# Attention scores on the two row halves of TensorE, memory products on whole tiles, and the order of a step around them

## The chip, the cores and the metric

One core of one Trainium2 chip. The metric is the device time of one launch in microseconds (us); the median of three runs of the kernel before is 1613.03 us. The engines are called by their names in the profile: PE is TensorE's matmuls and PEld its weight loads, DVE is VectorE, ACT is ScalarE, POOL is GpSimd, SP is the engine that issues the DMAs.

## The reference

Two branches read the same 2048 x 576 input `x`; a gate per row mixes them.

```python
g = sigmoid((x * gate_w).sum(-1, keepdims=True))
out = g * A(x) + (1 - g) * B(x)
B = (gelu(x @ w_gate) * (x @ w_up)) @ w_down          # 576 -> 4608 -> 576
# A: 32 heads of 18, four segments of 512 rows, in order
for s in range(4):
    p = softmax(q_s @ k_s.T * 18**-0.5 + mask)        # mask: keys ahead of the query
    a_dot = p @ v_s
    a_mem = (phi(q_s) @ M) / (phi(q_s) @ z + 1e-6)    # phi(t) = t + 1 or exp(t)
    o_s = sigmoid(beta) * a_mem + (1 - sigmoid(beta)) * a_dot
    M += phi(k_s).T @ v_s ; z += phi(k_s).sum(rows)
A = concat(o) @ wo
```

The mask leaves, for each of a segment's four query tiles of 128 rows (qi = 0 to 3), (qi + 1) x 128 keys.

## The kernel before, in words

Numbers are kept in pairs of 16-bit words (a high part and what is left), so most products come as several matmuls. Four stretches follow one another.

**Start and projections** (L594 to L823). The first segment's rows of `v` are made in full precision by `first_words`; the weights' scales come from sums of squares (`stat_v`, `stat_qk`, `scale_sum`, which sums over partitions by a small matmul at L90 into the bank that `spare` gives out). For each segment s, `vrows` makes the value rows, `project` makes nine tiles of columns (q in tiles 0 to 4, k in 4 to 8: tile 4 is shared, 64 rows each), and `put_columns` keeps phi of them. Every segment but the first also works on the memory of the one before, tile of 128 rows by tile (q): `key_rows` (L553) turns phi(k) to rows with transposes on TensorE, from tile 4's upper 64 rows on; `memorize` (L564) multiplies them with the values into two banks, where the fifth span of columns has 64 columns only; `keep_memory` (L574) masks that to head blocks in `bd`; `recall` (L517) multiplies phi(q) with `bd` into two banks of 16 heads each, so that the span that holds head 14 to 21 is cut in two and the fifth span has 64 rows only; `put_recall` (L534) divides and stores. Closures in the list `later` hold the second halves of these steps, and `finish_later` runs them; so the place of that call sets the order on VectorE.

**The main loop** (L1104, `step(v)`, 72 steps). A step is one tile of 128 hidden columns f for one half of the rows: V, X and Y are three banks (tags V, G, U), filled by seven half-products (`product`, `rest`, `low_rests`). Each step also does eight chains of the down projection of the block before (`down`, L977: six matmuls at L985, then one VectorE instruction at L991 or L993 that adds the bank to `acc`), in order: five `early` chains, one each after products X, S2 and A12 and two behind the even scores, then three `late` chains behind the fourth product (S4). A chain's bank comes from `spare()`, which in the loop means the two banks of tag `dn`. And each step carries one head of attention, with a lag of two steps:

- `scores(2k)` behind the first pair of low rests and `scores(2k+1)` at the end of the step. Its four query tiles are matmuls of 54 rows (three words of 18): qi = 3 on rows 0 to 53 in one `st` bank, qi = 2 and qi = 0 on rows 64 to 117 in the other, qi = 1 on rows 0 to 53 in a `dn` bank. `put(a, i)` (L896) reads piece i on VectorE: it adds the mask, keeps a copy in SBUF and the row maximum.
- `powers`, `pair_rows`, `turn_rows`: exponentials on ScalarE, the high and low words, and two transposing DMAs on SP's queue from `ph` to `pt` (two buffers each).
- `values(a)`: twenty matmuls of 37 columns at L940 into the bank `pv`; `normalize(k)`: five VectorE instructions (L950 to L957) that read `pv`. There is one `pv` bank, so the next head's `values` wait for it.

`end_pair` at the start of a step multiplies the two hidden tiles of the step before (L1007 on VectorE, from banks G and U) and splits them (L1011, L1012). The order on TensorE, ScalarE, VectorE and GpSimd is that of the code (`manual_schedule`); SP's queue is ordered by the compiler. PSUM is eight banks: G, U, V, pv, two `st`, two `dn`. A tag with two buffers gives a new tile the buffer that comes free first.

**The tail** finishes the last block's chains and the product with `wo`.

In the tile names of the profile `gl` is a gelu tile, `hh` its pair, `pairg` and `paird` are pairs of weights, `pf` the scores in SBUF, `mx` their maxima, `ob` the rows of a group of heads.

Of the kernel before, what the change touches and what calls it, by code (L numbers as in the profile page):

```python
# [8 lines left out]
F32 = mybir.dt.float32  # L9
# [9 lines left out]
P = 128  # L19
# [18 lines left out]
SPANS = [(128 * j, min(128, D - 128 * j)) for j in range(KT)]  # L38
HEADS = [(a // DH, (a + w - 1) // DH + 1) for a, w in SPANS]


@with_exitstack
def kernel(ctx: ExitStack, tc: tile.TileContext, xs, wqk, wv, wo, wgu, wd, beta, out):
# [346 lines left out]
    with tc.tile_pool(name="prj", bufs=2, side="right", reuse_waits="tile") as pp:  # L390
# [25 lines left out]
        def square_sum(o, r, on_act):  # L416
            if on_act:
                junk = pa.tile([P, D], F32, name="krow", bufs=2).bitcast(BF16)
                act.activation(junk[:, : r.shape[1]], r, AF.Square, accum_out=o)
            else:  # L420
                sum_squares(o, r)
# [4 lines left out]
        def stat_qk(j):  # L426
            square_sum(wst[:, 10 + j : 11 + j], raw_qk[:, j], j % 2)
# [89 lines left out]
        def recall(s, q, banks=(("st", 2), ("st", 2))):  # L517

            na, nb = (bank(*i) for i in banks)
            for j, (a, w) in enumerate(SPANS):  # L520
                h0, h1 = HEADS[j]
                for o, lo in ((na, 0), (nb, 16)):
                    g0, g1 = max(h0, lo), min(h1, lo + 16)
                    if g0 >= g1:
                        continue
                    last = (j == 2 and lo == 0) or j == KT - 1
                    first = j == 0 or (j == 2 and lo == 16)
                    pe.matmul(o[:, (g0 - lo) * MC : (g1 - lo) * MC],
                              phi[s, j][:w, q * P : (q + 1) * P],
                              bd[:w, j, (g0 - h0) * MC : (g1 - h0) * MC],  # L530
                              start=first, stop=last, skip_group_check=True)
            later.append(lambda: put_recall(s, q, na, nb))

        def put_recall(s, q, na, nb):  # L534
# [3 lines left out]
            for b, o in enumerate((na, nb)):  # L538
                o3 = o[:, : 16 * MC].rearrange("p (h d) -> p h d", d=MC)
                dve.tensor_scalar(dn[:, 16 * b : 16 * b + 16].unsqueeze(2), o3[:, :, DH:], 1e-6, None, OP.add)  # L540
            rd = pp.tile([P, H], F32, name="rden", bufs=2)
            mo = pp.tile([P, D], F32, name="mo", bufs=2)
            dve.reciprocal(rd, dn)
            dve.tensor_tensor(rd, rd, gh[:, 0], OP.mult)
            for b, o in enumerate((na, nb)):
                o3 = o[:, : 16 * MC].rearrange("p (h d) -> p h d", d=MC)
                dve.tensor_tensor(
                    mo[:, b * NH : (b + 1) * NH].rearrange("p (h d) -> p h d", d=DH),
                    o3[:, :, :DH],
                    rd[:, 16 * b : 16 * b + 16].unsqueeze(2).to_broadcast([P, 16, DH]), OP.mult)  # L550
            sp.dma_start(oms[hf][t * P : (t + 1) * P, :], mo)

        def key_rows(s, q):  # L553
            ka, kb = bank("st", 2), bank("V")
            tok = slice(q * P, (q + 1) * P)
            pe.transpose(ka[:, 0:64], phi[s, 4][64:, tok], ident[64:, 64:])
            for i in range(3):
                pe.transpose(ka[:, 64 + i * P : 64 + (i + 1) * P], phi[s, 5 + i][:, tok], ident)
            pe.transpose(kb[:, :P], phi[s, 8][:, tok], ident)
            k = kr[s, q] = pa.tile([P, D], F32, name="krow", bufs=2)  # L560
            act.activation(k[:, :448], ka[:, :448], AF.Copy)
            act.activation(k[:, 448:], kb[:, :P], AF.Copy)

        def memorize(s, q):  # L564
# [3 lines left out]
            for j, (a, w) in enumerate(SPANS):  # L568
                h0, h1 = HEADS[j]
                o = mem[s][j // 3][:w, (j % 3) * 8 * MC : (j % 3) * 8 * MC + (h1 - h0) * MC]  # L570
                pe.matmul(o, k[:, a : a + w], v[:, h0:h1].rearrange("p h d -> p (h d)"),
                          start=q == 0 and j % 3 == 0, stop=q == 3 and j in (2, 4), skip_group_check=True)

        def keep_memory(s):  # L574
            ka, kb = mem.pop(s)
            n = 8 * MC
            for o, d, k in ((ka[:, : 3 * n], flat(bd[:, 0:3]), flat(bdm[:, 0:3])),
# [4 lines left out]
                else:  # L582
                    m = pa.tile([P, D], F32, name="krow", bufs=2)[: o.shape[0], : o.shape[1]]
# [10 lines left out]
        with tc.manual_schedule(engines=ORDERED):  # L594
# [34 lines left out]
            stat_qk(4)  # L629
            low_x(0, 1)  # L630
            for j in (6, 5, 8, 7):
                stat_qk(j)
            finish_later()
            low_x(0, 2)
# [198 lines left out]
    with tc.tile_pool(name="keep", bufs=2, side="right", reuse_waits="tile") as kp, ExitStack() as tail:  # L833
# [262 lines left out]
        def end_pair():  # L1096

            for g in ends:
                hidden(*g)
# [229 lines left out]
```

## Time and profile before

| | |
|---|---|
| median of 3 runs | 1613.03 us (1612.63 to 1613.62) |
| the profiled execution's own time | 1610.65 us |
| its span | 1608.9 us |
| busy: PE, PEld | 1596.7, 933.5 us |
| busy: DVE, ACT, POOL | 1140.2, 1161.9, 1133.1 us |
| mean granted clock of TensorE | 0.998 |
| score matmuls (L888) | 4 x 128, of 512, 384, 256 and 128 columns |
| DMA queue 1 | 206.92 MB, 71.6% of 16 engines |

Lines of a timeline read: start (us from the span's start), length, engine, line of the code, operation, tile written <- tiles read, shape, count of instructions merged into the row; in brackets the engine's idle time before it and what ended it. Matmuls overlap: a row's start says when one began, the start of the next when it made room; the length includes the way through the array. A busy PE is therefore not yet a PE at its peak, and the spacing of starts is what is added up here. In the table of stretches the columns are the stretch, its length, the busy time (and count) of PE, PEld, DVE, ACT and POOL, the granted clock of TensorE, the busy share of the DMA engines and GB/s.

### The profile page before, as it was taken

How to read it: one execution, taken by the hardware profiler on the slowest of the kernel's cores; microseconds unless marked ns; L12 is line 12 of the kernel's file. 1: busy time of each engine (PE TensorE's matmuls, PEld its weight loads, DVE VectorE, ACT ScalarE, POOL GpSimd, SP SyncE). 2: the span in 40 equal slices, each digit the busy share in tenths (PEclk: the TensorE clock that was granted, in tenths of full speed). 3: DMA queues.
4: the chain of work that ended last, by engine and by line, in shares of the span. 5: the costliest groups of instructions: out<-in, count | busy, mean ns of one | idle time of the engine just before them, and what ended most of it. 6: DMA issues, size and time to landing. Idle time of an engine off the chain costs nothing.

```text
span 1608.9 us, 32610 instructions
## 1 busy us (share of the span) xinstructions
PE 1596.7 (99%) x11924; PEld 933.5 (58%) x11924; DVE 1140.2 (71%) x2940; ACT 1161.9 (72%) x1966; POOL 1133.1 (70%) x1093
## 2 busy tenths in 40 slices
PE   9999999999999999999999999999999999999999
PEld 5656754555555555555555555555555555555577
DVE  6665785677777777777777777777777777765543
ACT  6665445888888888888888888878888888864200
POOL 2233647798987888887979778888879797785200
PEclk9999999999999999999999999999999999999999
DMA  6532443788978797988988887978798887846251
GB/s 240 193 109 77 149 142 82 124 133 131 138 120 141 122 144 120 143 126 140 134 135 133 131 139 123 148 128 141 129 140 137 133 133 129 127 74 155 59 133 60
DMA packets 471872, 209.00 MB, mean 130 GB/s; under 512 B 427552, under 2 KB 436768, under 8 KB 471200
## 3 DMA queue, kind: packets, MB, share of 16 engines
q1 hardware_dynamic: 471712, 206.92, 71.6%
q8 instruction: 94, 1.54, 0.4%
q14 instruction: 66, 0.54, 0.1%
HBM read 90.99 MB, written 27.26 MB: 73 GB/s over the span
## 4 chain that ended last, share of the span: by engine, by line
PE 96%; DVE 1%; DMA 1%; POOL 1%; ACT 1%; issue 0%; SPq 0%; DVEq 0%; POOLq 0%
PE dn L985 26%; PE U L1025 17%; PE V L1025 12%; PE G L1025 11%; PE pv L940 4%; PE st L322 3%; PE st L312 3%; PE dn L322 2%; PE G L312 2%; PE U L1032 2%; PE st L888 2%; PE V L1037 1%; PE G L1037 1%; PE U L312 1%; PE G L1032 1%; PE V L1032 1%
## 5 line engine op out<-in xcount | busy, mean ns | idle before, releaser
L920 POOL TENSOR_TENSOR ph<-pf,ph 128x512 f16<-128x512 f32 (+1 forms) x256 | 354.2, 1405 | 176.9 <-ACT ph L919 175.0
L985 PE MATMUL dn<-paird,hh 128*128 128x288 f16 x3396 | 476.7, 286 | 0.9 <-POOL paird L305 0.9
L1025 PEld LDWEIGHTS <-pairg 128*128 128x128 f16 x3024 | 285.3, 98 | 309.9 <-issue 16.0
L985 PEld LDWEIGHTS <-hh 128*128 128x128 f16 x3456 | 332.3, 98 | 138.1 <-issue 2.6
L993 DVE SCALAR_TENSOR_TENSOR acc<-dn,ev,acc 128x288 f32<-128x288 f32 x534 | 274.0, 516 | 95.7 <-PE dn L985 86.9
L909 ACT ACTIVATE pf<-pf,mb,esc 128x512 f32<-128x512 f32 (+3 forms) x512 | 292.9, 642 | 6.7
L1025 PE MATMUL G<-x,pairg 128*128 128x512 f16 x864 | 209.9, 379 | 0.5 <-DVE gl L1007 0.5
L1025 PE MATMUL U<-xt,pairg 128*128 128x512 f16 x864 | 210.1, 379 | 0.0
L1012 POOL TENSOR_TENSOR hh<-gl,hh 128x512 f16<-128x512 f32 x144 | 164.0, 1160 | 56.0 <-ACT hh L1011 56.0
L896 DVE CUSTOM_DVE_ANT_0 pf<-st,mask 128x512 f32<-128x512 f32 (+2 forms) x384 | 184.0, 504 | 0.0
L293 POOL TENSOR_TENSOR pairg<-raw,pairg 128x640 f16<-128x640 f32 (+2 forms) x144 | 173.9, 1229 | 10.6 <-ACT pairg L289 10.6
L919 ACT ACTIVATE ph<-pf 128x512 f16<-128x512 f32 (+1 forms) x256 | 172.4, 720 | 0.0
L1162 DVE COPY gl<-U 128x512 f32<-128x512 f32 x72 | 49.8, 691 | 137.2 <-PE U L1025 137.2
L289 ACT ACTIVATE pairg<-raw 128x640 f16<-128x640 f32 (+2 forms) x144 | 89.5, 648 | 70.7 <-POOL raw L283 41.2
L258 POOL TENSOR_SCALAR raw<-raw,sc 128x640 f32<-128x640 f32 x72 | 135.0, 1889 | 0.0
L1015 ACT ACTIVATE gl<-gl,sc 128x512 f32<-128x512 f32 x144 | 98.3, 717 | 45.4 <-DVE gl L1181 25.2
L1025 PE MATMUL V<-x,pairg 128*128 128x512 f16 x432 | 106.0, 381 | 0.4 <-ACT hh L1011 0.2
L1181 DVE TENSOR_TENSOR gl<-U,gl 128x512 f32<-128x512 f32 x72 | 49.7, 691 | 79.8 <-PE U L1037 72.5
L1025 PE MATMUL V<-xt,pairg 128*128 128x512 f16 x432 | 105.7, 381 | 0.0
L1025 PE MATMUL U<-x,pairg 128*128 128x512 f16 x432 | 105.0, 379 | 0.4 <-DVE gl L1181 0.4
L1011 ACT ACTIVATE hh<-gl 128x512 f16<-128x512 f32 x144 | 82.9, 616 | 25.2 <-DVE gl L1007 25.1
L906 ACT ACTIVATE mb<-mx,esc 128x4 f32<-128x4 f32 x128 | 37.8, 295 | 85.8 <-DVE mx L896 83.1
(271 smaller groups left out, 2565.1 us busy)
## 6 DMA issues: line engine op xcount, KB each, us to landing
raw<-in_wgu_dram SPq DMA_DIRECT2D x36, 640.0 KB
rawd<-in_wd_dram SPq DMA_DIRECT2D x36, 288.0 KB
qk<-stage SPq DMA_DIRECT2D x36, 256.0 KB
qt<-qk SPq DMA_DIRECT2D x128, 72.0 KB
kt<-qk SPq DMA_DIRECT2D x128, 72.0 KB
vp<-vstage SPq DMA_DIRECT2D x16, 296.0 KB
vt<-vp SPq DMA_DIRECT2D x16, 296.0 KB
qt<-qk SPq DMA_DIRECT2D x128, 36.0 KB
```

What stands on the lines that cost most here:

```text
L258: pool.tensor_scalar(r, r, scl[f // 2][0][:, 0:1], None, OP.mult)
L293: pool.tensor_tensor(spot(f, *p, 1), raw_g[f][:, p[0] : p[1]], spot(f, *p, 0), OP.subtract)
L312: pe.matmul(o, w(k, a), x[:, 4 * b + k], start=n == 0, stop=False)
L896: dve.tensor_tensor_reduce(prob[a][:, COL[qi] : COL[qi + 1]], ov, mask[:, L - (qi + 1) * P :], 1.0, -3e38, OP.add, OP.max, mx[a][:, qi : q ...
L909: act.activation(r, r, AF.Exp, bias=b[:, qi : qi + 1], scale=esc[:, 0, c : c + 1])
L919: act.activation(h[:, 0, cols], p[:, cols], AF.Copy)
L920: pool.tensor_tensor(h[:, 1, cols], p[:, cols], h[:, 0, cols], OP.subtract)
L985: pe.matmul(o[:, :NH], hh[:, a, q * P : (q + 1) * P], w[:, b, n * NH : (n + 1) * NH], start=i == 0, stop=i == 5)
L993: dve.scalar_tensor_tensor(av, o[:, :NH], ev, av, OP.mult, OP.add)
L1012: pool.tensor_tensor(hh[:, 1], t, hh[:, 0], OP.subtract)
L1015: act.activation(t, o, AF.Gelu_apprx_tanh, scale=scl[f // 2][0][:, 2 + c : 3 + c])
L1025: pe.matmul(o, w[:, i, (a + k) * P : (a + k + 1) * P], x[:, b + k], start=start and k == 0 and i == 0 and b == h, stop=k == 1 and i == 1, ...
```

## The change

1. **Scores.** The four query tiles get a bank each: 3 and 2 in `st`, 1 and 0 in `dn`. Tiles 3 and 0 are on the lower rows (640 columns together), tiles 2 and 1 on the upper (640).
2. **Order in a step.** VectorE reads pieces 0 and 1 first, as they hold `dn` banks: those of the even scores right behind them, those of the odd scores in `end_pair`, between the two hidden tiles. `values(2k-3)` moves from the first half of the step to behind the even scores, `normalize(k-2)` from the middle of the step to behind the last piece of the even scores, `values(2k-2)` from behind the even scores to behind the late chains. In step 4 alone (the fifth) the first early chain moves to the second one's place.
3. **Memory.** `recall` uses all 128 rows and whole spans: three spans in one bank, two in the other. Head 21 then lies in both; `put_recall` copies its 19 columns from the second bank and adds them to the first. `key_rows` transposes six whole tiles, `memorize` uses 128 columns for each span. The mask `bdm` is in BF16, the unused rows of `bd` are set to zero, `krow` is 640 columns wide.
4. **Start.** The square sum of tile 6 moves to ScalarE. `finish_later` is cut into single calls. The scale of the q and k weights is made behind the first two value tiles' first halves on ScalarE, its sum goes to a `dn` bank, bank G is freed ahead of the first weight pair, and the third low part of `x` comes later.

```diff
 def stat_qk(j):
-    square_sum(wst[:, 10 + j : 11 + j], raw_qk[:, j], j % 2)
+    square_sum(wst[:, 10 + j : 11 + j], raw_qk[:, j], j in (1, 3, 5, 6, 7))
...
 def recall(s, q, banks=(("st", 2), ("st", 2))):
     na, nb = (bank(*i) for i in banks)
-    for j, (a, w) in enumerate(SPANS):
-        h0, h1 = HEADS[j]
-        for o, lo in ((na, 0), (nb, 16)):
-            g0, g1 = max(h0, lo), min(h1, lo + 16)
...
-            pe.matmul(o[:, (g0 - lo) * MC : (g1 - lo) * MC],
-                      phi[s, j][:w, q * P : (q + 1) * P],
-                      bd[:w, j, (g0 - h0) * MC : (g1 - h0) * MC],
-                      start=first, stop=last, skip_group_check=True)
+    for j, (h0, h1) in enumerate(HEADS):
+        o, lo = (na, 0) if j < 3 else (nb, HS)
+        pe.matmul(o[:, (h0 - lo) * MC : (h1 - lo) * MC], phi[s, j][:, q * P : (q + 1) * P],
+                  bd[:, j, : (h1 - h0) * MC], start=j in (0, 3), stop=j in (2, 4), skip_group_check=True)
...
 def put_recall(s, q, na, nb):
+    both = na[:, HS * MC : (HS + 1) * MC]
+    dve.tensor_copy(mo[:, :MC], nb[:, :MC])
+    dve.tensor_tensor(both, both, mo[:, :MC], OP.add)
...
 def key_rows(s, q):
-    pe.transpose(ka[:, 0:64], phi[s, 4][64:, tok], ident[64:, 64:])
-    for i in range(3):
-        pe.transpose(ka[:, 64 + i * P : 64 + (i + 1) * P], phi[s, 5 + i][:, tok], ident)
-    pe.transpose(kb[:, :P], phi[s, 8][:, tok], ident)
-    k = kr[s, q] = pa.tile([P, D], F32, name="krow", bufs=2)
-    act.activation(k[:, :448], ka[:, :448], AF.Copy)
-    act.activation(k[:, 448:], kb[:, :P], AF.Copy)
+    for i in range(4):
+        pe.transpose(ka[:, i * P : (i + 1) * P], phi[s, 4 + i][:, tok], ident)
+    for i, j in ((0, 8), (1, 4)):
+        pe.transpose(kb[:, i * P : (i + 1) * P], phi[s, j][:, tok], ident)
+    k = kr[s, q] = pa.tile([P, KT * P], F32, name="krow", bufs=2)
+    act.activation(k[:, :448], ka[:, 64:], AF.Copy)
+    act.activation(k[:, 448:], kb[:, :192], AF.Copy)
...
 def memorize(s, q):
-        o = mem[s][j // 3][:w, (j % 3) * 8 * MC : (j % 3) * 8 * MC + (h1 - h0) * MC]
-        pe.matmul(o, k[:, a : a + w], v[:, h0:h1].rearrange("p h d -> p (h d)"),
+        o = mem[s][j // 3][:, (j % 3) * 8 * MC : (j % 3) * 8 * MC + (h1 - h0) * MC]
+        pe.matmul(o, k[:, a : a + P], v[:, h0:h1].rearrange("p h d -> p (h d)"),
...
-            stat_qk(4)
+            for j in (4, 5, 6, 8, 7):
+                stat_qk(j)
+            later.pop(0)()
             low_x(0, 1)
-            for j in (6, 5, 8, 7):
-                stat_qk(j)
-            finish_later()
-            low_x(0, 2)
+            later.pop(0)()
...
                     if qs[0] and k == 1:
-                        scale_sum(0, wst[:, 10:19])
-                        make_qk(0)
                         put_rows(0, 0, 1, vb[0], usc, 1.0)
                         put_rows(0, 1, 1, vb[1], usc, 1.0)
+                        turns.update(of=2)
+                        scale_sum(0, wst[:, 10:19])
+                        turns.update(of=3)
+                        later.pop(2)()
+                        make_qk(0)
+                        low_x(0, 2)
                         finish_later()
...
-        PIECES = (((3,), 0), ((2, 0), 64), ((1,), 0))
+        PIECES = ((3, 0, "st"), (2, 64, "st"), (1, 64, "dn"), (0, 0, "dn"))
...
+            for qi, r, tag in PIECES:
+                n, h = (qi + 1) * P, slice(r, r + 3 * DH)
+                out[qi] = bank(tag, 2)[:, :n]
+                pe.matmul(out[qi], q[h, e * L + qi * P : e * L + n], kt[h, e * L : e * L + n], start=True, stop=True)
...
         def end_pair():
             for g in ends:
                 hidden(*g)
+                if g is ends[0]:
+                    for qi in (0, 1):
+                        if puts:
+                            puts[max(puts)](qi)
...
         def step(v):
...
             product(X, f, A11, x1, 0, 4, True)
-            put(2 * k - 1, 0)
+            put(2 * k - 1, 3)
             dve.tensor_copy(Y, X)
...
-            some(fb - 1, early[:1])
-            put(2 * k - 1, 1)
+            if v != 4:
+                some(fb - 1, early[:1])
             put(2 * k - 1, 2)
             puts.pop(2 * k - 1, None)
-            if on(k - 2):
-                values(2 * k - 3)
...
-            some(fb - 1, early[1:2])
+            some(fb - 1, early[0 if v == 4 else 1 : 2])
...
-            if on(k - 2):
-                normalize(k - 2)
             product(X, f, A12, x1, 2, 6)
...
             if on(k):
                 puts[2 * k] = scores(2 * k)
+            put(2 * k, 0)
+            put(2 * k, 1)
             dve.tensor_tensor(g1, Y, g1, OP.add)
             gelu(f, e, g1, g1)
...
-            put(2 * k, 2)
             if fb:
                 dve.tensor_tensor(g0, V, g0, OP.add)
                 gelu(f, c, g0, g0)
-            if on(k - 1) and fb:
-                values(2 * k - 2)
+            if on(k - 2):
+                values(2 * k - 3)
             some(fb - 1, early[3:4])
-            put(2 * k, 0)
+            put(2 * k, 3)
             some(fb - 1, early[4:])
-            put(2 * k, 1)
+            put(2 * k, 2)
             puts.pop(2 * k, None)
+            if on(k - 2):
+                normalize(k - 2)
...
             product(Y, f, S4, x2_, 2, 6)
             rest(Y, f, UG, x2_, (0,) if fb else (0, 1))
             some(fb - 1, late[:1])
...
             some(fb - 1, late[1:])
-            if on(k - 1) and not fb:
+            if on(k - 1):
                 values(2 * k - 2)
```

49 lines of the change are left out of this document (18 added, 31 removed).

## The prediction

> **What bounds the kernel now.** I read the page's head and its chain that ended last, then the table of busy time by stretch, then the timelines of TensorE and VectorE over one step of the main loop, at last VectorE's waits.
>
> ```profile
> span 1608.9 us, 32610 instructions
> ...
> PE 96%; DVE 1%; DMA 1%; POOL 1%; ACT 1%; issue 0%; SPq 0%; DVEq 0%; POOLq 0%
> ```
>
> TensorE is 96% of the chain. Its own queue is the time; any other engine matters only where TensorE must wait for it. So I look at one step in the middle, and ask how much room each wait leaves. TensorE (S below is the start of the even head's scores, 808.66):
>
> ```profile
> 797.21 1.47 PE L1025 MATMUL V<-xt,pairg 128*128 128x512 f16 x6
> ```
>
> ```profile
> 808.44 0.39 PE L1037 MATMUL U<-x,pairg 64*128 64x512 f16 x1
> 808.66 0.38 PE L888 MATMUL st<-kt,qt 54*128 54x512 f16 x3
> 808.88 0.27 PE L888 MATMUL dn<-kt,qt 54*128 54x256 f16 x1
> 809.08 0.67 PE L940 MATMUL pv<-vt,pt 128*128 128x37 f16 x20
> 809.60 1.63 PE L985 MATMUL dn<-paird,hh 128*128 128x288 f16 x12
> 811.07 1.46 PE L1025 MATMUL U<-x,pairg 128*128 128x512 f16 x6
> ...
> 812.58 2.40 PE L985 MATMUL dn<-paird,hh 128*128 128x288 f16 x18
> ...
> 815.56 1.47 PE L1025 MATMUL V<-xt,pairg 128*128 128x512 f16 x6
> ```
>
> The step lasts 18.35 us (797.21 to 815.56) and no row of it carries idle time. Six matmuls of a chain take 0.735 (twelve from 809.60 to 811.07), so the three late chains begin at 812.58, 813.31 and 814.05. VectorE beside it:
>
> ```profile
> 805.22 0.46 DVE L950 TENSOR_REDUCE pv<-pv 128x144 f32<-128x288 f32 x1
> ...
> 806.63 0.30 DVE L957 TENSOR_TENSOR ob<-ob,pv 128x144 f32<-128x144 f32 x1
> 807.03 0.52 DVE L993 SCALAR_TENSOR_TENSOR acc<-dn,ev,acc 128x288 f32<-128x288 f32 x1
> 808.87 0.69 DVE L1181 TENSOR_TENSOR gl<-U,gl 128x512 f32<-128x512 f32 x1 [1.32 <-PE U L1037]
> 809.48 0.41 DVE L896 CUSTOM_DVE_ANT_0 pf<-dn,mask 128x256 f32<-128x256 f32 x1
> ...
> 809.82 0.69 DVE L1189 TENSOR_TENSOR gl<-V,gl 128x512 f32<-128x512 f32 x1
> 810.53 0.52 DVE L993 SCALAR_TENSOR_TENSOR acc<-dn,ev,acc 128x288 f32<-128x288 f32 x1
> 810.97 0.68 DVE L896 CUSTOM_DVE_ANT_0 pf<-st,mask 128x512 f32<-128x512 f32 x1
> ...
> 811.57 0.51 DVE L993 SCALAR_TENSOR_TENSOR acc<-dn,ev,acc 128x288 f32<-128x288 f32 x1
> 812.00 0.54 DVE L896 CUSTOM_DVE_ANT_0 pf<-st,mask 128x384 f32<-128x384 f32 x1
> ...
> 812.48 0.28 DVE L896 CUSTOM_DVE_ANT_0 pf<-st,mask 128x128 f32<-128x128 f32 x1
> ...
> 813.51 0.52 DVE L993 SCALAR_TENSOR_TENSOR acc<-dn,ev,acc 128x288 f32<-128x288 f32 x1 [0.74 <-PE dn L985]
> ```
>
> Its rows stand in the order of the code. Two things are to be seen. The normalization (five instructions, 805.22 to 806.93) sits where VectorE would else be idle. And the sum of the first late chain ends at 814.03, while the third late chain wants to begin at 814.05: it can, just. The chains take turns in the two `dn` banks, so the third needs the bank that the first chain's sum gives back. There is no room left at this place. That it is so in nearly every step, the waits of VectorE tell (us in total, times, longest):
>
> ```profile
> DVE gl L1181 <- PE U L1037: 72.5, 63, 1.3
> ```
>
> **The change, part by part.**
>
> *Scores.* The second score matmul of the lower half starts 0.22 after the first (808.66 to 808.88) for 512 columns. The lower half has 768 columns now, 0.33, and then 0.09 to the next instruction at 809.08. With 640 columns in each half it is 0.275: 0.05 less in each of the 128 score blocks, 6.8 in all.
>
> *Order in a step.* This is where the price lies. Both small pieces of the scores now go to `dn`, so both `dn` banks are taken, and VectorE reads them first (`put(2k,0)`, `put(2k,1)`). `values(2k-3)` moves behind the even scores, the normalization therefore behind the last piece, and `values(2k-2)` behind the late chains. Nothing is added in instructions but one; but on VectorE the normalization now stands ahead of the late chains' sums. From S, by the rows above:
>
> - first piece: the last score result is there at S+0.49 (the row at 808.88 with its 0.27 ends so; the 128 columns start no later), and VectorE takes 0.04 to start (808.83, the end of L1037, to 808.87): 0.5 or a little under.
> - pieces 0.21 (that of 812.48, with the accumulator read starting 0.21 later) and 0.34 (809.48 to 809.82), the two additions 0.61 and 0.65, first early sum 0.44, 512 piece 0.60, second early sum 0.43, 384 piece 0.48, normalization 1.65. Sum 5.41: the first late sum starts at S+5.9 and ends at S+6.42.
> - TensorE without waits: `values` starts at S+0.37 (0.42 today, less 0.05) and takes 0.52 (809.08 to 809.60), so the two early chains start at S+0.89 and end 1.47 later at S+2.36; product and rest take 1.51 (811.07 to 812.58), so the late chains start at S+3.87, 4.61 and 5.34.
>
> So the third late chain waits from S+5.34 to S+6.45, 1.1 us. Today it starts at S+5.39. Per step that is 1.07 more, less 0.05 for the odd scores, whose saving still shows (that of the even ones is swallowed by this wait): **1.0 us a step**. Behind the waiting chain, TensorE's queue holds `values`, the low rests and the odd scores, and all of the next step: nothing overtakes. What is late next? The odd scores need the banks of the second and third late sums; these end some 0.3 before that, also where the result's low half (L969) stands between. The first early chain needs the first piece's bank at S+0.89, against a read done at about S+0.8; if it is late, the 1.1 shrinks by as much, for the end of VectorE's row does not move. ScalarE's exponentials start as before, since the last piece ends near 812.9. The transposing DMAs of an odd head now wait for `values(2k-3)`, and SP's queue behind them holds heads and weights for later steps; their readers moved back by as much or more, so I take nothing. With 62 such steps (the 63 waits above, less one at the edge): +62. Bounds: VectorE's rows overlap by up to 0.08 each, so the wait is 0.85 to 1.25, that is +50 to +75.
>
> *Memory's products.*
>
> ```profile
> 115.06 0.27 PE L556 MATMUL st<-ident,phi 64*128 64x64 f32 x1
> 115.26 0.55 PE L558 MATMUL st<-ident,phi 128*128 128x128 f32 x3
> 115.64 0.27 PE L559 MATMUL V<-ident,phi 128*128 128x128 f32 x1
> 115.75 1.82 PE L528 MATMUL st<-bd,phi 128*128 128x152 f32 x12
> 117.50 1.65 PE L322 MATMUL dn<-wv,x 128*128 128x290 f16 x12
> ...
> 119.24 0.94 PE L571 MATMUL U<-v,krow 128*128 128x152 f32 x6
> 120.02 0.70 PE L571 MATMUL pv<-v,krow 128*128 128x152 f32 x4
> 120.65 0.54 PE L322 MATMUL dn<-wv,x 128*128 128x288 f16 x3
> ```
>
> A recall takes 1.75 (115.75 to 117.50) for fourteen passes in two row shapes. One pass of 152 columns is 0.13 (six from 119.24 to 120.02); after the change there are eight of these and two of half the width, 1.17: 0.58 less, twelve times. Memorizing takes 1.41 (119.24 to 120.65) and will take the same 1.17: 0.24 less, twelve times. The transposes take 0.69 with the 64-row one and become six of 0.11, some 0.66, and the 64-row change ahead of them goes: 0.1 less. Together 11. What eats it: the recall gets two small VectorE instructions, ScalarE copies 64 columns more.
>
> ```profile
> 108.00:137.00 29.00, 29.00 (x216) 23.19 (x214) 20.85 (x46) 13.55 (x29) 6.92 (x11) 1.00 0.34 121
> ...
> 199.00:230.00 31.00, 31.00 (x162) 17.15 (x160) 28.89 (x54) 18.42 (x28) 18.54 (x16) 1.00 0.37 120
> ```
>
> (Columns: stretch, length, busy PE, PEld, DVE, ACT, POOL, clock, DMA.) VectorE is busy 20.9 of 29 in the first stretch, which covers it, but 28.9 of 31 in the second, where three recalls stand. So 10.5, between 6 and 12. The narrower mask and the wider `krow` tile change no instruction's count.
>
> *The start.*
>
> ```profile
> 24.47 0.36 PE L90 MATMUL V<-wst,ones 128*128 128x9 f32 x2 [0.87 <-DVE vstage L494]
> ...
> 28.90 2.75 PE L312 MATMUL G<-x,wp 128*128 128x512 f16 x12 [1.33 <-DVE gate L496]
> ```
>
> The two idle times are 2.2. With the sum in a `dn` bank the first goes. The second product then waits for a bank that VectorE frees at the end of the same list of work, which has begun 0.87 earlier: I take 0.9, between 0 and 2.2; the one square sum that goes over to ScalarE is within that.
>
> *The fifth step.* Deferring its first chain and both `values` lets operands arrive.
>
> ```profile
> 282.73 0.69 PE L940 MATMUL pv<-vt,pt 128*128 128x37 f16 x19 [0.84 <-DMA pt<-ph]
> ...
> 294.10 0.64 PE L940 MATMUL pv<-vt,pt 128*128 128x37 f16 x19 [0.89 <-DMA pt<-ph]
> ```
>
> ```profile
> 283.00:287.00 4.00, 4.00 (x25) 1.58 (x22) 0.45 (x4) 3.31 (x7) 2.59 (x2) 0.57 0.64 194
> 293.00:297.00 4.00, 3.10 (x37) 2.23 (x38) 2.78 (x9) 3.17 (x5) 3.97 (x4) 1.00 0.88 174
> ```
>
> The two waits for transposed rows are 1.73; behind the first (and two of 0.18 and 0.71 for the down weights, just before) the clock stood at 0.57 for 4 us, which lost 0.43 of it, 1.7. I take 3.5 of the sum of 4.3, since the second transfer may still come last; between 0 and 5.
>
> *Sum.* 1608.9 + 62 (steps) − 10.5 (memory) − 0.9 (start) − 3.5 (fifth step) = 1656. The profiled execution took 1610.65, 1.75 more than its span, and the median of the runs shown is 1613.03, 2.4 above that one; so I add the same 47 to the median: **1660**.
>
> **One rule of the Trainium skill** speaks against this change more than I do. "TensorE: Matmul & The Clock Gate", section "A second HAM failure mode: psum-queue depth-cycling", says that a kernel whose TensorE idles briefly between groups of matmuls, as it cycles through PSUM banks, can have its clock swing between half and full. The trace agrees for three waits close together (0.57 above) and disagrees for one wait of 0.89 by itself, behind which it stayed at 1.00 (293 to 297). By that rule the sum would be that of the second rival below; by the rows it is mine.
>
> **The rivals.**
>
> 1. *Faster: the bank is free in time.* Then only the gains are left: 6.8 + 10.5 + 0.9 + 3.5 = 21.7, so 1591. The place is the first late sum; the mechanism is that VectorE gets to it by S+4.85, as it does now (813.51), because the normalization doesn't in fact stand ahead of it, or overlaps with its neighbours. It holds in full from the point where VectorE's list is 1.1 shorter than I add it. For it: VectorE idles 1.32 before L1181 and 0.74 before the late sum, 2.06 together, which is more than the 1.65 moved. Against it: only the 0.74 and about 0.4 of the 1.32 lie where the moved work can use them, and each row of VectorE stands in the order of the code.
> 2. *Much slower: the clock drops in each step.* A wait of 1.1 in every 19 us, each followed by what 283 to 287 shows: 1.7 lost per step, 62 times, +105 on mine: 1765. For it: that stretch. Against it: 293 to 297.
> 3. *No change: the wait is a third of mine.* At 0.35 a step the 62 steps cost 22, and the gains pay for it: 1613. For it: the overlap of VectorE's rows goes that way. Against it: it would take 0.7 of overlap in twelve instructions whose starts I read off the trace, overlap included.
> 4. *The halves don't run side by side* any better than before: no gain of 0.05 a block. The even half is swallowed anyway; the odd one is 3.3: 1663, inside my range.
>
> **How the numbers follow.** My forecast has 0.80: 1660, by itself 1640 to 1680 (steps +50 to +75, memory 6 to 12, start and fifth step 0 to 7). Rival 1 has 0.12, rival 2 has 0.05, rival 3 has 0.03; rival 4 is counted within mine. The range is to leave out no more than 0.2, which the forecast's own range just does; I widen it for waits that I have not seen to 1630 to 1690. 0.2% of the time is 3.2 us, about what a measurement of this kernel can tell from no change. So: faster 0.12, same 0.03, slower 0.85.
>
> **What would show it.** In the changed profile a step in the middle lasts 19.35 and not 18.35; its only idle time on TensorE is one of about 0.9 to 1.0 before an L985-like row of the down chains, ended by VectorE's sum into `acc`, and VectorE no longer idles before that sum. The waits would list TensorE waiting for `acc` some 62 times. The score block lasts 0.37 from its first start to the next instruction, a recall 1.2, memorizing 1.2. The fifth step has no wait for `pt` early on. If the step lasts 18.25, rival 1 holds and my list for VectorE was wrong; if the clock by stretch falls under 1.00 in the loop, rival 2; if TensorE's idle time stands before the first early chain, I have the wrong bank. The forecast is wrong too if the memory stage gives nothing because VectorE is behind in 199 to 230.

## The result and the profile after

| | before | after |
|---|---|---|
| median of five runs each, us | 1612.63 (1611.5 to 1613.62) | 1660.04 (1658.68 to 1661.5) |
| span of the profiled execution, us | 1608.9 | 1658.0 |

The changed kernel takes 1.0295 times as long (95% interval 1.028 to 1.031). The head of its page and its chain that ended last:

```profile
span 1658.0 us, 32537 instructions
...
PE 72%; DVE 24%; issue 1%; DMA 1%; ACT 1%; POOL 0%; SPq 0%; DVEq 0%; POOLq 0%; ACTq 0%
```

VectorE had 1% of this chain and has 24% now. That does not mean that VectorE costs 24%: once in each step the chain crosses to VectorE, and followed back it then runs along VectorE's list for some 6 us, until TensorE's results release that. What it costs is the time for which TensorE stands still. The timeline of TensorE over one step of the changed kernel (columns as before; of the first row two records are missing in the trace):

```profile
776.28 1.04 PE L1020 MATMUL V<-xt,pairg 128*128 128x512 f16 x4
...
787.23 0.38 PE L888 MATMUL st<-kt,qt 54*128 54x512 f16 x2
787.40 0.27 PE L888 MATMUL dn<-kt,qt 54*128 54x256 f16 x2
787.60 0.67 PE L935 MATMUL pv<-vt,pt 128*128 128x37 f16 x20
788.12 1.63 PE L980 MATMUL dn<-paird,hh 128*128 128x288 f16 x12
...
791.10 1.63 PE L980 MATMUL dn<-paird,hh 128*128 128x288 f16 x12
793.64 0.90 PE L980 MATMUL dn<-paird,hh 128*128 128x288 f16 x6 [0.91 <-DVE acc L988]
...
795.57 1.47 PE L1020 MATMUL V<-xt,pairg 128*128 128x512 f16 x6
```

The step lasts 19.29 (776.28 to 795.57). The late chains begin at 791.10, and two of 0.735 later, at 792.57, the third could begin: it does at 793.64, so it waits 1.07. The row's own 0.91 is less, because the matmul before it still counts as busy on its way through the array. With S = 787.23, VectorE beside it:

```profile
787.75 0.29 DVE L891 CUSTOM_DVE_ANT_0 pf<-dn,mask 128x128 f32<-128x128 f32 x1 [1.63 <-PE dn L888]
...
788.91 0.68 DVE L1185 TENSOR_TENSOR gl<-V,gl 128x512 f32<-128x512 f32 x1
789.51 0.51 DVE L988 SCALAR_TENSOR_TENSOR acc<-dn,ev,acc 128x288 f32<-128x288 f32 x1
...
791.45 0.46 DVE L945 TENSOR_REDUCE pv<-pv 128x144 f32<-128x288 f32 x1
...
792.85 0.30 DVE L952 TENSOR_TENSOR ob<-ob,pv 128x144 f32<-128x144 f32 x1
793.08 0.93 DVE L988 SCALAR_TENSOR_TENSOR acc<-dn,ev,acc 128x288 f32<-128x288 f32 x2
```

From 787.75 to 793.08 VectorE has no idle time: pieces, additions, early sums, and then the normalization (791.45 to 793.08). Only behind it comes the first late sum, whose bank the third late chain needs. In the waits (us in total, times, longest) it stands as

```profile
PE dn L980 <- DVE acc L988: 52.6, 58, 0.9
```

and in the table of stretches the granted clock (third column from the end) stays at full in the loop, in spite of these waits:

```profile
400.00:480.00 80.00, 76.38 (x624) 44.22 (x623) 55.33 (x157) 63.89 (x105) 64.65 (x60) 1.00 0.72 124
```

Where the 49.1 us of span come from, by the first matmul of steps 0, 4, 5 and 66 in both traces:

| stretch | before | after | difference |
|---|---|---|---|
| up to step 0 | 229.71 | 221.88 | −7.83 |
| steps 0 to 3 | 47.11 | 51.71 | +4.60 |
| step 4 (the fifth) | 23.73 | 19.39 | −4.34 |
| steps 5 to 65 | 1122.03 | 1178.66 | +56.63 |

61 steps with 0.93 more each are all of the loss. Ahead of them 7.57 are won in sum: the start and the memory part win 7.83, steps 0 to 3 give 4.60 of it back, and step 4 wins 4.34.

### The profile page after: what moved, and what is told of

Same layout as the page of the kernel before. It is cut to its first block, busy times and chain, and to the rows that moved or that the text cites. A ratio compares the mean times of both kernels' runs of the same rounds, so it can differ in the third digit from the quotient of the medians.

```text
span 1658.0 us, 32537 instructions
## 1 busy us (share of the span) xinstructions
PE 1586.4 (96%) x11912; PEld 939.9 (57%) x11912; DVE 1126.7 (68%) x2962; ACT 1166.6 (70%) x1968; POOL 1133.9 (68%) x1094
## 4 chain that ended last, share of the span: by engine, by line
PE 72%; DVE 24%; issue 1%; DMA 1%; ACT 1%; POOL 0%; SPq 0%; DVEq 0%; POOLq 0%; ACTq 0%
PE dn L980 15%; PE U L1020 12%; PE V L1020 11%; PE G L1020 11%; DVE pf L891 6%; DVE acc L988 5%; PE st L323 3%; DVE pv L949 2%; DVE gl L1178 2%; DVE gl L1185 2%; PE pv L935 2%; PE st L313 2%; DVE pv L945 1%; PE dn L323 1%; PE V L1032 1%
## 5 line engine op out<-in xcount | busy, mean ns | idle before, releaser
L980 PE MATMUL dn<-paird,hh 128*128 128x288 f16 x3396 | 484.1, 286 | 56.2 <-DVE acc L988 52.6
L1020 PEld LDWEIGHTS <-pairg 128*128 128x128 f16 x3024 | 290.2, 98 | 311.9 <-issue 15.8
L988 DVE SCALAR_TENSOR_TENSOR acc<-dn,ev,acc 128x288 f32<-128x288 f32 x534 | 268.2, 512 | 129.4 <-PE dn L980 128.9
L891 DVE CUSTOM_DVE_ANT_0 pf<-st,mask 128x512 f32<-128x512 f32 (+1 forms) x256 | 156.6, 612 | 0.0
L891 DVE CUSTOM_DVE_ANT_0 pf<-dn,mask 128x128 f32<-128x128 f32 (+1 forms) x256 | 80.7, 353 | 106.3 <-PE dn L888 106.3
L1006 ACT ACTIVATE hh<-gl 128x512 f16<-128x512 f32 x144 | 88.0, 621 | 35.0 <-DVE gl L1002 34.8
```

Source lines behind the costliest of these rows:

```text
L891: dve.tensor_tensor_reduce(prob[a][:, COL[qi] : COL[qi + 1]], out[qi], mask[:, L - (qi + 1) * P :], 1.0, -3e38, OP.add, OP.max, mx[a][:, q ...
L980: pe.matmul(o[:, :NH], hh[:, a, q * P : (q + 1) * P], w[:, b, n * NH : (n + 1) * NH], start=i == 0, stop=i == 5)
L988: dve.scalar_tensor_tensor(av, o[:, :NH], ev, av, OP.mult, OP.add)
L1020: pe.matmul(o, w[:, i, (a + k) * P : (a + k + 1) * P], x[:, b + k], start=start and k == 0 and i == 0 and b == h, stop=k == 1 and i == 1, ...
```

## The experiments

Theory 1: the loss is the place of the normalization in VectorE's list, ahead of a sum that gives back a `dn` bank. Rivals: the new banks of the scores lose it; VectorE has too much to do wherever the normalization stands; the memory part or the start lose it. Line numbers are those of the kernel quoted.

### The loop alone, and all but the loop

`new_loop` is the kernel before with the changed `scores`, `end_pair` and `step`; `old_loop` is the changed kernel with these three functions as before.

```diff
 # new_loop, two of its places
-        PIECES = (((3,), 0), ((2, 0), 64), ((1,), 0))
+        PIECES = ((3, 0, "st"), (2, 64, "st"), (1, 64, "dn"), (0, 0, "dn"))
...
-            if on(k - 2):
-                normalize(k - 2)
             product(X, f, A12, x1, 2, 6)
...
             puts.pop(2 * k, None)
+            if on(k - 2):
+                normalize(k - 2)
```

> Scores and the order of a step as changed, memory's products and the start as before. Theory 1: steps of 19.29, 61 of them 57 us dearer, the fifth 4 cheaper: 1663 to 1668. Theory 2 gives the same here. If the changed start or memory had a part in the loss: below 1655.

Measured: 1665.22 us, 1.0326 (1.0309 to 1.0344) of before, as expected. Its trace shows one more price of the new order, in step 3, which lasts 16.55 where the kernel before has 15.03:

```profile
275.46 1.46 PE L1018 MATMUL U<-x,pairg 128*128 128x512 f16 x6 [1.46 <-DVE gl L1176]
```

The kernel before waits 0.36 at this place, and `old_loop` 0.35. The sum awaited, VectorE's for the second gelu, stands behind the two score pieces that the new order puts ahead of it; `early_g1` (below) moves it.

> Memory's products and the start as changed, scores and the order of a step as before. If the two halves of the change are separate: what the changed kernel had gained when its loop began, 7.8 us, less what the first steps may take back (0 to 3), so 1604 to 1608, with steps of 18.36. If VectorE's backlog from the recalls takes the gain back in the first steps: 1609 to 1613.

Measured: 1608.19 us, 0.9977 (0.9967 to 0.9986). The loop holds all of the loss, and the other parts win 3.9 us, about at the border of my two expectations. Its step 0 begins at 221.25, 8.46 earlier than before, but it has only 3.15 left where step 5 begins (297.40): step 0 gives back 2.0, step 3 1.2 and step 4 2.1. TensorE's timeline in step 4 shows how:

```profile
286.89 0.19 PE L942 MATMUL pv<-vt,pt 128*128 128x37 f16 x1 [1.40 <-DMA pt<-ph]
...
289.71 0.78 PE L942 MATMUL pv<-vt,pt 128*128 128x37 f16 x19 [2.63 <-DMA pt<-ph]
```

Before, the longest such wait was 0.89. The transposed rows did not come earlier by as much as TensorE did. (In step 0 TensorE waits 1.60 for VectorE here.)

### A shorter normalization

```diff
-for i in range(2):
-    b = slice(4 * i, 4 * i + 4)
-    dve.scalar_tensor_tensor(sm[:, b], sm[:, b], gha[:, 2 * hf + i, k : k + 1], ...)
-dve.tensor_tensor(od, od, sm, OP.add)
+dve.scalar_tensor_tensor(od, sm, gha[:, 2 * hf, k : k + 1], ...)
```

> The changed kernel, but the normalization ends with one VectorE instruction over all eight row tiles that writes the head's rows, in place of two multiplications and an addition (left out: the memory's part of the output, and the second segment's own scale). Theory 1 (the third late chain waits for VectorE's list, in which the normalization stands ahead of the first late sum): the list is about 0.6 us shorter, so the wait of 1.07 falls to about 0.45, the step from 19.29 to about 18.65, and the time from 1660 to 1620 to 1626. Theory 2 (the wait comes from the two small score pieces taking both dn banks, the normalization hides in it): step and time stay within 0.1 and 5 us.

Measured: 1621.76 us, 1.0056 (1.0036 to 1.0076). TensorE's row:

```profile
795.12 0.90 PE L977 MATMUL dn<-paird,hh 128*128 128x288 f16 x6 [0.29 <-DVE acc L985]
```

The place is the same and the wait is shorter: 0.29 where the changed kernel has 0.91. The normalization lasts 1.03 there (793.53 to 794.56) where it lasted 1.63: 0.60 less VectorE time gave 0.62 less wait, and most steps went from 19.28 to 18.67. So over this range what stands ahead of that sum is paid in full. The banks of the scores are the same as in the changed kernel, and the step moved by 0.61: theory 2 is out. (`norm_short` leaves out the memory's part of the output and the second segment's own scale.)

### The normalization moved by one place

```diff
             if on(k - 2):
                 values(2 * k - 3)
+                normalize(k - 2)
             some(fb - 1, early[3:4])
...
             puts.pop(2 * k, None)
-            if on(k - 2):
-                normalize(k - 2)
```

> The changed kernel with the normalization moved by one place only: directly behind the odd half's values product, still ahead of the last two early sums in VectorE's list. Theory 1 (any bank of the tag dn whose sum stands behind the normalization is late, there by VectorE's sums for the gelus as well): the late chains wait nearly as much in sum, split over two or three of them, 1645 to 1662 us. Rival (only the first late sum may not stand behind it): the wait goes, 1592 to 1600 us.

Measured: 1661.36 us, 1.0303 (1.0284 to 1.0321), as theory 1 has it. The late chains:

```profile
985.08 0.38 PE L1027 MATMUL U<-x,pairg 128*128 128x512 f16 x1
985.91 2.83 PE L980 MATMUL dn<-paird,hh 128*128 128x288 f16 x18 [0.45 <-DVE acc L988]
```

A matmul of 512 columns makes room after 0.216 (1.30 for six), so the first late chain is 0.61 late, and the eighteen matmuls last 2.83 where the kernel before had 2.40: the same microsecond, now in three waits. The waits of TensorE list only 25.7 us in all for it, half of the changed kernel's, at nearly the same total time: idle time alone would have misled here, and only the spacing of starts tells.

### The normalization in the first half of the step

From step 5 on, `norm_mid` puts values and normalization back at the places that they had before the change and issues the even scores ahead of S1; `norm_early` leaves the scores as changed and puts values and normalization together ahead of the product A22.

```diff
 # both: ahead of A22
             puts.pop(2 * k - 1, None)
+            if on(k - 2) and v != 4:
+                values(2 * k - 3)
+                normalize(k - 2)          # norm_early
 # norm_mid: normalize(k - 2) ahead of A12 instead, and
+            low_rests(f, (V, G4, x1), (Y, G4, x2_))
+            puts[2 * k] = scores(2 * k)
             product(Y, f, S1, t, 0, 2)
```

> The changed kernel, but from step 5 on the odd head's values and the normalization stand where they stood before, and the low rests and the even scores are issued ahead of the product S1, which then covers the reading of the two dn pieces (the addition of g0 comes with it). Theory 1: nothing stands between the last piece and the first late sum, the wait goes back to the 0.05 of before, the step is 18.25 (18.39 in one of four), 1.03 less than 19.29, and the time 1597 (1594 to 1601): faster than both kernels. Theory 2: both dn banks are still taken by the pieces, and a wait of at least 0.5 stays: steps of 18.7 or more, 1625 or more.

Measured: 1628.44 us, 1.0098 (1.0083 to 1.0113). Theory 1 misses, though the late wait is gone; the number is theory 2's, but its reason is not what the trace shows. The scores follow directly on the third early chain now, and their last piece needs that chain's bank:

```profile
1055.24 0.27 PE L888 MATMUL dn<-kt,qt 54*128 54x256 f16 x1
1056.72 0.21 PE L888 MATMUL dn<-kt,qt 54*128 54x128 f16 x1 [1.21 <-DVE acc L988]
```

That sum stands behind the normalization, and in each fourth step behind the weights' scales too (L218 to L225), which makes it 1.2; the other steps last 18.48, about 0.2 more than the 18.29 of `norm_mid2` (below), where it is gone.

> The changed kernel with one thing put elsewhere: from step 5 on (and in steps 2 and 3) the odd half's values product and, directly behind it, the memory's normalization stand right after the second score piece of the odd half, ahead of the product A22, where VectorE idles 1.85 us before its next copy; scores, banks and chains stay as in the changed kernel. Theory 1 (the change loses by the place of the normalization in VectorE's list alone): the 1.07 us ahead of the third late chain goes, steps of 18.21 us (18.35 each fourth), 62 x 1.07 = 66 us less than the changed kernel: 1592 to 1598 us. Rival (VectorE's list is full, so the 1.65 us come back at another bank): a new wait of 0.2 us or more in each step, 1605 us or more.

Measured: 1626.67 us, 1.0088 (1.0074 to 1.0101). The late wait is gone here as well, and again another stands in its place:

```profile
980.41 0.27 PE L888 MATMUL dn<-kt,qt 54*128 54x256 f16 x2
981.11 1.63 PE L980 MATMUL dn<-paird,hh 128*128 128x288 f16 x12 [0.43 <-DVE mx L891]
```

The number is the rival's, but not its reason: VectorE's list is not full, as `both_moves` (below) shows. The early chain now follows directly on the score pieces, whose banks it takes. In the changed kernel the 0.5 us of `values` stood between the two and gave VectorE the time to read them.

### The third early chain behind S1, then both moves

`norm_mid2` is `norm_mid` with the third early chain behind S1 instead of ahead of the scores:

```diff
-            some(fb - 1, early[2:3])
             low_rests(f, (V, G4, x1), (Y, G4, x2_))
             puts[2 * k] = scores(2 * k)
...
             product(Y, f, S1, t, 0, 2)
...
+            some(fb - 1, early[2:3])
```

> As the kernel before it in this study (norm_mid: from the second pair on the memory's normalization and the odd half's values product stand where they stood before the change, and the even half's scores are issued ahead of the product S1), but the third early chain of the down projection now stands behind S1, so that the last score piece takes a bank whose sum stands ahead of the normalization in VectorE's list. Theory 1 (a step is lengthened only where a bank of the tag dn is released by a sum that stands behind the normalization or the scales): the waits of 0.17 us in every step and 1.2 us in each fourth step go, steps of 18.25 us (18.4 each fourth), 61 x about 1.0 us less than the changed kernel's steps of 19.28, so 1595 to 1601 us. Rival (VectorE has too much work between two chains wherever the normalization is put): another wait of 0.5 to 1 us appears in each step, 1625 us or more.

Measured: 1609.76 us, 0.9984 (0.9975 to 0.9994). Three steps of four last 18.28 and 18.29, near the 18.25 expected; each fourth, 19.06, is a miss, as is the total, which is the rival's just as little. There the scales and the normalization stand one behind the other ahead of the sums:

```profile
972.23 0.90 PE L980 MATMUL dn<-paird,hh 128*128 128x288 f16 x6 [0.34 <-DVE acc L988]
```

`both_moves` adds to this the place of the normalization that `norm_early` had, where VectorE idled 1.85 us, and the edit of `early_g1` (below).

> The changed kernel's memory, start, scores and banks, with the two moves that the earlier runs left standing, from step 5 on: the odd half's values product and the normalization right behind it ahead of the product A22 (as in norm_early), and the even half's scores ahead of S1 with the third early chain behind S1 (as in norm_mid2), so that no bank of the tag dn waits for a sum behind the normalization, and no chain follows directly on the score pieces; and in the first four steps the second gelu's sum ahead of the short pieces (as in early_g1). Theory 1: no wait in a step, 18.2 to 18.3 us (18.35 to 18.4 each fourth), 16 waits of 0.74 us fewer than norm_mid2 and about 1 us less in step 3: 1595 to 1599 us. Rival (VectorE's list in each fourth step is too long with the scales in it, wherever the normalization stands): steps of 18.7 us or more each fourth, 1604 us or more.

Measured: 1598.36 us, 0.9912 (0.9899 to 0.9926), faster than both kernels. From step 6 to the end of the loop TensorE's timeline has no idle time left but one wait of 0.27 at 1449.03, which the kernel before has too (at 1459.26). The late chains of one step:

```profile
804.20 2.40 PE L980 MATMUL dn<-paird,hh 128*128 128x288 f16 x18
806.44 0.66 PE L935 MATMUL pv<-vt,pt 128*128 128x37 f16 x20
```

The late chains last 2.40 as before the change, and steps 18.28 to 18.42. So the normalization is no load that VectorE cannot carry (60.67 of 80 us busy between 800 and 880): it needed its early place and the third early chain its late one, and either alone carried the wait to another bank. The scores keep their new banks here, so the banks do not lose the time either.

`early_g1` is `norm_early` with one VectorE instruction earlier in steps 0 to 3:

```diff
+            if not fb:
+                dve.tensor_tensor(g1, Y, g1, OP.add)
             put(2 * k, 0)
             put(2 * k, 1)
-            dve.tensor_tensor(g1, Y, g1, OP.add)
+            if fb:
+                dve.tensor_tensor(g1, Y, g1, OP.add)
```

> norm_early, and in the first four steps alone VectorE's sum for the second gelu stands ahead of the even half's two short score pieces. In step 3 of the changed kernel TensorE waited 1.46 us at the product S4 for that sum. Theory (the sum is held up by the pieces that the change put ahead of it): 0.5 to 1 us less than norm_early. Rival (steps 3 and 4 wait for the transposed probabilities anyway): within 0.4 us of norm_early.

Measured: 1626.05 us against 1626.67 of `norm_early`; the ranges of the two overlap, so the total decides nothing. In the traces step 3 went from 17.42 to 16.08 us, so the wait of 1.46 there was the order's; step 5 lasted 0.28 longer (19.15 against 18.87).

### The split of the scores

`norm_mid2`, with the columns shared between the halves of rows as before the change:

```diff
-PIECES = ((3, 0, "st"), (2, 64, "st"), (1, 64, "dn"), (0, 0, "dn"))
+PIECES = ((3, 0, "st"), (2, 64, "st"), (1, 0, "dn"), (0, 64, "dn"))
```

> norm_mid2 with the score pieces given to the halves as before the change (512 and 256 columns to rows 0 to 53, 384 and 128 to rows 64 to 117) but each in its own bank as after it. Theory (the two halves of rows run side by side, and a block lasts as long as the half with more columns: 768 against 640 columns, 0.053 us): 132 blocks of 0.05 us more, 7 us more than norm_mid2 (5 to 8). Rival (the halves do not run side by side, so the split is worth nothing): within 1.5 us of norm_mid2.

Measured: 1614.23 us, 4.5 more than `norm_mid2`: below the 5 to 8 expected, and beyond the rival's 1.5. A score block with the old split, then one in `norm_mid2`:

```profile
970.77 0.38 PE L888 MATMUL st<-kt,qt 54*128 54x512 f16 x2
...
971.19 1.47 PE L1020 MATMUL U<-xt,pairg 128*128 128x512 f16 x6
```

```profile
977.53 0.38 PE L888 MATMUL st<-kt,qt 54*128 54x512 f16 x2
...
977.90 1.47 PE L1020 MATMUL V<-xt,pairg 128*128 128x512 f16 x6
```

0.42 against 0.37: the 0.05 a block are there, and steps are 18.39 against 18.29. In each fourth step the wait of `norm_mid2` takes them up (19.06 in both): 45 steps of 0.10 are the 4.5, where all blocks had been counted.

### Memory and start one by one

`mem_only` is the kernel before with `recall`, `put_recall`, `key_rows`, `memorize`, the mask and `krow` as changed, `start_only` with the square sums and the order of the start as changed.

```diff
 # start_only
-    square_sum(wst[:, 10 + j : 11 + j], raw_qk[:, j], j % 2)
+    square_sum(wst[:, 10 + j : 11 + j], raw_qk[:, j], j in (1, 3, 5, 6, 7))
...
 # mem_only
-        pe.matmul(o, k[:, a : a + w], v[:, h0:h1].rearrange("p h d -> p (h d)"),
+        pe.matmul(o, k[:, a : a + P], v[:, h0:h1].rearrange("p h d -> p (h d)"),
```

> The kernel before with the changed memory part alone (recall, memorizing, transposes of keys), with the start and the steps as before. Theory 1 (what TensorE gains ahead of step 0 is mostly given back by step 4, where the values product waits for transposed probabilities): step 0 begins 7 to 8 us earlier, but the end comes only 3 to 4 us earlier, 1608.5 to 1610 us. Rival (nothing behind it holds the gain back): 1604 to 1606 us.

Measured: 1609.64 us, 0.9986 (0.9977 to 0.9996), in the range of theory 1, but 2.4 us less and not the 3 to 4 expected. Step 0 begins 5.95 earlier (223.76), less than the 7 to 8 expected.

> The kernel before with the changed order at the start alone (which squares ScalarE takes, the first scale's place). The prediction gave it 0.9 us (0 to 2.2) ahead of the memory part. Theory 1: step 0 begins 0.5 to 1 us earlier and the end comes 0 to 0.6 us earlier, 1612 to 1612.7 us. Rival (it is worth its full part): 1611.5 us or less.

Measured: 1611.15 us, 0.9993 (0.9983 to 1.0003). The figure lies in the rival's range (1611.5 or less), but it is only 0.86 below the 1612.01 of the kernel before that was measured beside it, and not to be told from nothing; step 0 begins 0.58 earlier (229.13). In `mem_only` the stretches of step 4 show how the gain goes:

```profile
290.00:294.00 4.00, 1.34 (x23) 1.06 (x24) 0.00 (x0) 3.25 (x5) 3.97 (x4) 0.57 1.27 174
294.00:298.00 4.00, 4.00 (x17) 2.11 (x16) 2.32 (x8) 0.21 (x1) 0.00 (x0) 0.58 0.17 34
```

TensorE waits for the transposed rows (1.34 of 4 us busy), and the clock over these eight microseconds is 0.57 and 0.58. That profiled execution took 1611.57, the longest of this kernel's runs, so its size is not that of the median. SP's queue shows where part of the gain is lost. The second transposing DMA of the first head took 2.99 (from 268.35) where the kernel before has 1.33 (from 272.30). The pair that TensorE awaits in step 4 stands behind it in that queue and began 2.95 earlier than before (283.09 against 286.04), while TensorE reached the scores ahead of it 4.69 earlier (287.77 against 292.46). Why that one DMA took longer was not tried and stays open.

## Why the prediction was right, and where not

The time was right by a right mechanism, and to the last microsecond by luck: two errors of opposite sign nearly cancel.

- **What bounds, and the late wait: right.** The place (the third late chain), the cause (the first late sum behind the normalization) and the clock times are those that were worked out: first late sum at S+5.9 predicted and at S+5.85 measured (793.08), third late chain at S+6.45 and S+6.41. `norm_short` shows it by dose, `norm_up` by place, `both_moves` by taking it away; `new_loop` shows that the loss lies in the loop.
- **1.0 a step, 62 steps: mis-sized, 0.93 in 61.** By parts of the step: from its first matmul to S 11.45 became 10.95, from S to the third late chain 5.39 became 6.41, from there to the next step 1.51 became 1.93. By the prediction's terms these would be −0.52, +1.06 and +0.47, and they are −0.50, +1.02 and +0.42. So +56.6 and not +62; inside the +50 to +75.
- **The scores' 0.05 a block: right** (`split_old`: 0.42 and 0.37). That the halves do run side by side settles the fourth rival.
- **Memory −10.5: mis-sized.** The instructions cost nearly what was said: a recall and a memorizing last 1.21 each (113.77 to 114.98, 116.71 to 117.92) where 1.17 was worked out. But TensorE now runs ahead of the other engines there, and not only in the stretch that the prediction warned of. TensorE's timeline of the changed kernel:

```profile
113.08 0.63 PE L555 MATMUL st<-ident,phi 128*128 128x128 f32 x4 [0.48 <-DVE mo L546]
113.55 0.38 PE L557 MATMUL V<-ident,phi 128*128 128x128 f32 x2
113.77 1.38 PE L524 MATMUL st<-bd,phi 128*128 128x152 f32 x10
114.98 1.64 PE L323 MATMUL dn<-wv,x 128*128 128x290 f16 x12
...
216.36 1.45 PE L524 MATMUL dn<-bd,phi 128*128 128x152 f32 x10 [0.77 <-DVE mo L546]
...
224.94 1.45 PE L1020 MATMUL G<-x,pairg 128*128 128x512 f16 x6 [1.61 <-DVE stage L472]
...
269.76 1.46 PE L1020 MATMUL U<-x,pairg 128*128 128x512 f16 x6 [1.46 <-DVE gl L1178]
...
272.64 0.64 PE L935 MATMUL pv<-vt,pt 128*128 128x37 f16 x19 [0.82 <-DMA pt<-ph]
```

  The waits at 113.08 and 216.36 fall into the memory part; with two more there (0.47 at 62.11, 0.86 at 168.81) they are 2.6 where the kernel before has none. The third falls into step 0, and `mem_only` has it too (1.61 at 226.83; step 0 lasts 11.20 in both, 9.21 before). Of the two in step 3, the wait for `pt` belongs to the memory's gain (0.77 in `old_loop`, none in `new_loop`), but the 1.46 (0.36 before) to the new order, as `new_loop` shows.

  With the start, 11.4 were to be won ahead of step 0; 7.83 were, of which steps 0 to 3 gave back 4.60: 2.0 in step 0 and 2.7 in step 3. Two steps of the prediction are wrong here. It summed a stage's gains to its end and asked for the cover inside it, but not who would be late behind it. And it took the price of the new order from 62 steps and put nothing for the four ahead of them, where step 3 alone costs 1.5 (16.55 in `new_loop` against 15.03).
- **Start −0.9: not settled by its run.** In `start_only` the two waits at the start, 2.20 together, are one of 1.24 (at 30.63), 0.96 less. Step 0 begins 0.58 earlier; but ten of the kernels quoted have the changed start and memory, and their step 0 begins anywhere from 221.22 to 222.74, so 0.58 in one execution tells little.
- **Fifth step −3.5:** 4.34 less in that step. Its waits for `pt` and for the down weights are gone, and the clock stays at 1.00 (283 to 287); one wait of 0.93 for a late sum (at 291.06) is new.
- **The sum:** steps 62 against 56.6, gains 14.9 against 7.6; +47 against +49.1 in span. That the median fits better still (1660 against 1660.04) is luck once more: the profiled execution of before lies 2.4 below its median, that of after at its median.
- **Rivals.** The first would have needed the bank in time. Its 1591 was too low even then: with no such wait left, `both_moves` takes 1598.4, and the 7.4 between them are close to the 7.3 of gains that did not arrive. The second, for which the Trainium skill's "TensorE: Matmul & The Clock Gate" was cited (section "A second HAM failure mode: psum-queue depth-cycling"), did not occur: with a wait of 1.07 in each step the clock is 1.00 (400 to 480). The third is out by the 1.07 (it needed 0.35).

## What to carry to other kernels

When an instruction is moved on an engine that works in order, look for the first instruction behind it that gives a buffer back, and compare its end with the moment at which the next user of that buffer would start; the engine's busy share (68% here) says nothing of that. Then ask the same of what the moved work used to separate: two moves, of which each alone only carried the wait to another bank, together (and with a small one in the first four steps) made the changed kernel 0.9% faster than the one before. And a gain ahead of a stage is worth what is left of it at the end: run it alone, and read the same point of both traces further and further down.

## What the runs showed of the hardware

Which waits of TensorE make its clock fall was bracketed by chance. In the changed kernel the 1.61 at 224.94 left the clock at 1.00 from 224 to 232, as did the waits of 1.07 in each step, and so did 1.46 and 0.82 within 4.3 us in step 3:

```profile
224.00:228.00 4.00, 2.98 (x14) 1.28 (x14) 3.86 (x13) 0.00 (x0) 0.00 (x0) 1.00 0.60 205
...
269.00:273.00 4.00, 2.42 (x23) 1.14 (x23) 2.56 (x9) 3.97 (x6) 4.00 (x4) 1.00 1.21 145
```

In the profiled execution of `both_moves`, the longest of its five, one wait of 1.96 in step 5 (it ended at 300.34, by a sum of squares on ScalarE) did not:

```profile
296.00:300.00 4.00, 2.38 (x14) 1.15 (x12) 1.40 (x5) 3.94 (x9) 3.79 (x4) 1.00 0.50 103
300.00:304.00 4.00, 3.66 (x16) 1.29 (x17) 2.69 (x9) 3.91 (x9) 3.76 (x6) 0.70 0.60 106
304.00:308.00 4.00, 4.00 (x24) 2.35 (x23) 2.83 (x9) 3.06 (x5) 4.00 (x5) 0.88 0.88 122
```

The clock was 0.70 and 0.88 in the next eight microseconds, which lost (0.30 + 0.12) × 4 = 1.7 of them, nearly as much as the wait itself. The length of one wait is not all that counts: in the kernel before the clock fell to 0.57 (283 to 287) behind waits of 0.18, 0.71 and 0.84 within 2.7 us, each of them shorter than 1.61. No run varies the waits alone, so where the limit lies stays open.
